# A second layer in three units of 192, 192 and 128 columns, and first keys scaled in halves

## The chip, the cores and the metric

The kernel runs on one core of a Trainium2 chip. The metric is the device time of one execution in microseconds; the kernel before takes 358.3 us (median of three runs, 358.1 to 358.67). TensorE (PE in the rows) multiplies matrices into PSUM, VectorE (DVE) and ScalarE (ACT) work on SBUF and PSUM, GpSimd (POOL) on SBUF, and SyncE (SP) issues the DMAs, which sixteen DMA engines carry out.

## What is computed

Attention on 8 batches of 8 heads (576 tokens, 64 columns a head, a mask by blocks of 64 tokens), and a soft mixture of experts on its output:

```python
scores = scale * q @ k.T                        # masked by blocks of 64
x = softmax(scores) @ v                         # as 4608 rows of 512
logits = x @ phi                                # 4608 x 32: 8 experts x 4 slots
slot_input = softmax(logits, over the rows).T @ x
h = relu(slot_input[e] @ w1[e])                 # 4 x 1024 for each expert
slot_out[e] = h @ w2[e]                         # 4 x 512
out = softmax(logits, over the slots) @ slot_out
```

All numbers are float32. `out` has 4608 rows of 512 columns; in the kernel it is written turned, 1152 rows of 2048 numbers, and the host turns it back.

## The kernel before

The attention goes over 32 pairs of heads, m = 0 to 31, as one list of steps in a fixed order: `at(t, fn, ...)` puts each step at a time (lines 843 to 937), the list is sorted, and each engine works it off in that order. Queries, keys and values come by `load_q`, `load_k` and `load_v`; `scale_k` multiplies the keys by 0.125 on GpSimd; `qk` and `qkb` form the scores. For the first pair this is the start of the kernel: SyncE issues keys, queries, the next keys, the next queries and the values, one after the other. Until the first keys are scaled, TensorE runs `WARM` = 8 matmuls on zeros (`warm`), and VectorE builds `stack` and `own` (lines 247 to 256), small constants that the second half uses.

The weights lie in `w`, 32 pieces of 128 x 2048 numbers (1 MB): 16 of the first layer, 16 of the second. 18 are loaded during the attention, 7 more into buffers that the last pairs leave (`places`), and the last 7 by `use(i)`, which reuses the buffer of a piece of the first layer as soon as that has been multiplied. The first layer (`up`, line 1064) takes 4 x 4 rounds.

The second layer (`down`, line 1082) goes by units: `NU` = 4 units of `CW` = 128 of the 512 columns. A unit is 16 steps; a step is four matmuls side by side, each of 128 rows by 32 columns of the array, over 128 columns of weights. When a unit is done, VectorE copies its sums to SBUF (`so_sb`), `finish(u)` adds the four strips up on TensorE (`summed`), and ScalarE copies the result (`s4[u]`). Then `emit(u, i)` forms parts of the output: `c` (the softmax over the slots, turned, in `cT`) for 2048 tokens (i = 0 and 1, the two token halves) against the 128 columns of the unit, four matmuls of 32 rows by 128 columns of the array side by side, 512 tokens each, into four banks of PSUM. ScalarE and VectorE copy two banks each to a staging buffer (one of the first layer's buffers that is free), and SyncE sends it: unit 0 as one DMA of 1 MB a part, later units as two of 512 KB, each after the second of its two copies. The last 512 tokens of all units go as parts '12' and '32', two units each. The order of the whole ending is written out in `ENDING` (line 63): a number is so many steps of `down` for the units behind unit 0, 'f1' is `finish(1)`, '10' is `emit(1, 0)`. The parts take turns in four banks ("x"); the last unit uses other banks as well. An engine works in its written order, so a copy that waits holds what is behind it on that engine.

Of the kernel before, what the change touches and what calls it, by code (L numbers as in the profile page):

```python
# [17 lines left out]
DM = H * D  # L18
# [22 lines left out]
WARM = 8  # L41
# [11 lines left out]
NPIECE = 32  # L53
# [177 lines left out]
def tile_attention_softmoe(  # L231
# [6 lines left out]
    w: bass.AP,  # L238
# [13 lines left out]
    for qd in range(2):  # L252
        for g in range(4):
            r = slice(NS * g, NS * (g + 1))
            s0 = 16 * qd + 4 * g
            nc.vector.tensor_reduce(out=own[r, qd:qd + 1], in_=stack[r, s0:s0 + 4], axis=AX.X, op=ALU.add)
# [51 lines left out]

    def load_piece(i, dst):
        place[i] = dst  # L310
        nc.sync.dma_start(out=dst, in_=w[i])
        pieces[i] = dst.rearrange("p (g f) -> p g f", g=4 if i < 16 else 16)
# [18 lines left out]
    with ExitStack() as c1:  # L331
# [91 lines left out]
        def scale_k(m):  # L423
            nc.gpsimd.tensor_scalar(  # L424
                out=area(f"ks{m % NQB}"), in0=area(f"ks{m % NQB}"), scalar1=SCALE, scalar2=0.0, op0=ALU.mult, op1=ALU.add
            )
# [515 lines left out]
    with ExitStack() as c2:  # L942
# [42 lines left out]
        def use(i):  # L985
# [3 lines left out]
            if fetched[0] < NPIECE:  # L989
# [19 lines left out]
        def emit(u, i):  # L1009
            ot = stage[no[0] % len(stage)]  # L1010
            no[0] += 1
            pss = []
            if (u, i) in ((NU - 1, 0), (NU - 1, 2)):
                pss += [nextbank("h") for g in range(2)]
                pss += [nextbank("so") for g in range(2, 4)]
            if (u, i) != (NU - 1, 2):
                pss += [nextbank("x") for g in range(4)]
            todo = [(s4[u], cT[:, i, 0:16, :])] if i < 2 else [(x, cT[:, :, 16:18, :]) for x in (s4[u - 1], s4[u])]
            m = 512 if i < 2 else 128
            n = m * len(todo)  # L1020
            lo = 256 * u + 128 * i
            if (u, i) == (NU - 1, 0):
                for h in range(2):
                    for g in range(4):
                        r = slice(NS * g, NS * (g + 1))
                        nc.tensor.matmul(
                            pss[4 * h + g][:, 0:256], lhsT=s4[u][r, :], rhs=cT[r, i, 8 * h:8 * h + 8, :],
                            start=True, stop=True, tile_position=(NS * g, 0),
                        )
                    for g in range(4):  # L1030
                        o = 1024 * h + 256 * g
                        (nc.vector.tensor_copy if g % 2 else nc.scalar.copy)(
                            out=ot[:, o:o + 256], in_=pss[4 * h + g][:, 0:256]
                        )
                        if g % 2:
                            nc.sync.dma_start(out=out[lo:lo + 128, o - 256:o + 256], in_=ot[:, o - 256:o + 256])
                return
            for x, (a, c) in enumerate(todo):
                for g in range(4):
                    r = slice(NS * g, NS * (g + 1))  # L1040
                    nc.tensor.matmul(  # L1041
# [123 lines left out]
```

## Time and profile before

| | |
|---|---|
| median of three runs | 358.3 us |
| the profiled execution: span | 357.1 us |
| around the span, in the median | 1.2 us |
| first scores start | 4.51 us |
| second layer starts | 320.48 us |
| first output sent | 328.01 us |
| last matmul of the output ends | 349.4 us |
| DMA queue falls idle | about 354.5 us |

The span runs from the first to the last instruction of the core. The rows that the prediction rests on stand in a section of their own below. In a row of the timeline the first number is the start, the second how long the group lasts, then engine, line, operation, tiles and shapes, the count, and in brackets how long the engine had been idle and what ended that. Each matmul on float32 stands as two records.

### The profile page before, as it was taken

Reading aid. Unit: us, or ns where it says so; the run is one execution under the profiler, and the core shown is the slowest. Engines: PE = TensorE matmul, PEld = TensorE weight load, DVE = VectorE, ACT = ScalarE, POOL = GpSimd, SP = SyncE. Lnnn points to the kernel's source line nnn. Section 1 sums busy time; section 2 is a strip of 40 time slices with the busy share of each in tenths; the row PEclk is TensorE's granted clock in tenths of the full one; section 3 lists DMA queues with packets and bytes.
Section 4 is the critical chain, followed back from the end, with each engine's and each line's share of the span. In section 5 each row is a group of like instructions: output and inputs, shape, how many; then the busy total and the mean of one; then the engine's idle time right before and its main releaser. Section 6 shows DMA issues by size and latency. Waiting matters only on the chain.

```text
span 357.1 us, 14425 instructions
## 1 busy us (share of the span) xinstructions
PE 342.2 (96%) x5724; PEld 237.1 (66%) x5724; DVE 261.5 (73%) x748; ACT 272.0 (76%) x869; POOL 205.0 (57%) x471
## 2 busy tenths in 40 slices
PE   8999999999999999999999999999999999999991
PEld 3767776677666766776767676776677677436750
DVE  4977777868887888777877887788888777462552
ACT  3988989888988898889888988899888875121441
POOL 3886767666766676567656766676687582000000
PEclk9999999999999999999999999999999999999996
DMA  6566526563664365743843556428333189999897
GB/s 198 182 211 229 163 74 212 199 225 101 184 224 133 102 218 186 249 106 114 292 135 101 204 195 211 148 70 312 127 104 102 36 253 331 375 397 397 327 373 298
DMA packets 29938, 72.29 MB, mean 202 GB/s; under 512 B 6960, under 2 KB 15280, under 8 KB 25520
## 3 DMA queue, kind: packets, MB, share of 16 engines
q1 hardware_dynamic: 29872, 71.38, 57.8%
q8 instruction: 45, 0.74, 0.8%
q14 instruction: 21, 0.17, 0.1%
HBM read 61.93 MB, written 9.44 MB: 200 GB/s over the span
## 4 chain that ended last, share of the span: by engine, by line
PE 79%; DVE 10%; POOL 5%; issue 3%; ACT 1%; DVEq 0%; POOLq 0%
PE one L592 15%; PE one L554 14%; PE one L464 7%; PE duo L464 7%; PE one L602 6%; PE one L485 5%; DVE stat L507 5%; POOL arena L534 4%; PE one L1088 4%; PE one L326 4%; PE duo L485 3%; PE one L1041 2%; PE one L623 2%; PE one L792 2%; DVE arena L392 1%
## 5 line engine op out<-in xcount | busy, mean ns | idle before, releaser
L534 POOL TENSOR_SCALAR arena<-arena,stat 128x512 f32<-128x512 f32 (+6 forms) x288 | 152.2, 544 | 30.8 <-DVE one L505 13.2
L517 ACT ACTIVATE arena<-one,stat 128x512 f32<-128x512 f32 (+5 forms) x194 | 93.9, 501 | 8.4 <-DVE stat L507 7.0
L390 ACT COPY arena<-one 128x384 f32<-128x384 f32 (+2 forms) x170 | 79.2, 503 | 26.8 <-PE one L554 21.3
L554 PEld LDWEIGHTS one<-ident,arena 64*128 64x128 f32 x1600 | 65.6, 138 | 33.4 <-ACT arena L390 9.0
L554 PE MATMUL one<-ident,arena 64*128 64x64 f32 x1600 | 76.3, 228 | 3.5 <-DVE arena L392 2.1
L507 DVE TENSOR_REDUCE stat<-one 128x1 f32<-128x512 f32 (+5 forms) x194 | 78.3, 436 | 1.7 <-PE one L485 0.6
L592 PE MATMUL one<-arena 128*64 128x256 f32 (+2 forms) x640 | 76.1, 384 | 0.0
L392 DVE COPY arena<-one 128x384 f32<-128x384 f32 (+3 forms) x106 | 56.4, 541 | 23.6 <-PE one L592 17.6
L517 ACT ACTIVATE arena<-duo,stat 128x384 f32<-128x384 f32 (+1 forms) x94 | 59.6, 640 | 7.0 <-DVE stat L523 5.6
L507 DVE TENSOR_REDUCE stat<-duo 128x1 f32<-128x576 f32 (+1 forms) x63 | 53.9, 855 | 13.3 <-PE duo L485 7.9
L592 PEld LDWEIGHTS one<-arena 128*64 128x64 f32 x640 | 41.1, 137 | 29.8 <-issue 18.2
L527 POOL TENSOR_SCALAR stat<-stat 128x2 f32<-128x2 f32 (+1 forms) x96 | 18.7, 195 | 55.0 <-ACT arena L517 50.9
L485 PE MATMUL one<-arena 64*64 64x256 f32 (+3 forms) x512 | 42.0, 303 | 0.0
L517 ACT ACTIVATION_READ_ACCUMULATOR arena<-one,stat 128x1 f32 x194 | 41.3, 213 | 0.0
L485 PE MATMUL duo<-arena 64*64 64x288 f32 x256 | 38.3, 417 | 0.0
L464 PE MATMUL one<-arena 64*128 64x512 f32 (+1 forms) x132 | 38.1, 636 | 0.0
L485 PEld LDWEIGHTS one<-arena 64*64 64x64 f32 x512 | 35.7, 133 | 2.2 <-ACT arena L517 0.4
L464 PE MATMUL duo<-arena 64*128 64x384 f32 x124 | 28.0, 529 | 0.4 <-ACT arena L517 0.4
L602 PE MATMUL one<-arena 128*64 128x64 f32 x620 | 24.9, 227 | 0.4 <-ACT arena L390 0.4
L602 PEld LDWEIGHTS one<-arena 128*64 128x64 f32 x620 | 20.6, 137 | 5.9 <-ACT xn L390 2.7
L424 POOL TENSOR_SCALAR arena<-arena 128x576 f32<-128x576 f32 x32 | 21.5, 672 | 3.6 <-DMA arena<-in_k 3.0
L523 DVE RECIPROCAL stat<-stat 128x2 f32<-128x2 f32 (+1 forms) x96 | 15.8, 165 | 7.2 <-POOL stat L527 6.9
(157 smaller groups left out, 382.8 us busy)
## 6 DMA issues: line engine op xcount, KB each, us to landing
arena<-in_w SPq DMA_DIRECT2D x31, 1024.0 KB, 7.2
arena<-in_k SPq DMA_DIRECT2D x32, 288.0 KB, 3.1
arena<-in_q SPq DMA_DIRECT2D x32, 288.0 KB, 3.2
arena<-in_v SPq DMA_DIRECT2D x32, 256.0 KB, 3.5
out<-arena SPq DMA_DIRECT2D x12, 512.0 KB, 4.5
out<-arena SPq DMA_DIRECT2D x2, 1024.0 KB, 5.6
arena<-in_v SPq DMA_DIRECT2D x32, 32.0 KB, 3.4
xarea<-in_w SPq DMA_DIRECT2D x1, 1024.0 KB, 8.0
```

The lines of the kernel that those rows point to most:

```text
L390: nc.scalar.copy(out=out, in_=in_)
L392: nc.vector.tensor_copy(out=out, in_=in_)
L424: nc.gpsimd.tensor_scalar(out=area(f"ks{m % NQB}"), in0=area(f"ks{m % NQB}"), scalar1=SCALE, scalar2=0.0, op0=ALU.mult, op1=ALU.add)
L464: nc.tensor.matmul(scores(t + str(j), m)[o, a:e], lhsT=q[r, lo + o.start:lo + o.stop], rhs=k[r, a:e], start=True, stop=True)
L485: nc.tensor.matmul(o, lhsT=a, rhs=b, start=True, stop=True)
L507: nc.vector.tensor_reduce(out=st[:, 0, u:u + n], in_=sc, axis=AX.XY if x == "8" else AX.X, op=ALU.max, negate=True)
L517: nc.scalar.activation(out=pr, in_=sc, func=AF.Exp, bias=st[:, 0, u:u + 1], accum_out=st[:, 1, u:u + 1],)
L527: nc.gpsimd.tensor_scalar(out=st[:, 2, c], in0=st[:, 1, c], scalar1=EPS, scalar2=1.0, op0=ALU.add, op1=ALU.mult)
L534: nc.gpsimd.tensor_scalar(out=pr, in0=pr, scalar1=st[:, 2, u:u + 1], scalar2=0.0, op0=ALU.mult, op1=ALU.add)
L554: nc.tensor.transpose(out=trbank(m, g)[i][:, 64 * n:64 * n + 64], in_=prob(m, x)[r, 128 * c:128 * c + 128], identity=ident[r, r],)
L592: nc.tensor.matmul(xps[m, 0][64 * j:64 * j + 64, lo:hi], lhsT=vs(m)[:, j, c, :], rhs=rhs, start=a, stop=z, skip_group_check=True,)
L602: nc.tensor.matmul(xps[m, 1][64 * j:64 * j + 64, 0:64], lhsT=vs(m)[:, j, c, :], rhs=arena[:, lo:lo + 64], start=(c == 0), stop=(c == NQ - 1),)
```

## The change

The second layer is cut into `UNITS` of 192, 192 and 128 columns. Steps of the units of 192 columns multiply 192 columns each. The weights of the second layer become 18 pieces in place of 16 (seven for a unit of 192: ten steps' slices of 192 columns to a piece, the last piece shorter), so nine are loaded by `use` in place of seven, and six staging buffers are left in place of eight. `finish` is called three times; for a unit of 192 ScalarE makes two copies, of 128 columns and of 64.

The parts are now: for each of the units of 192 two parts as before (128 columns, a token half each: '00', '01', '10', '11') and one of its last 64 columns with both token halves side by side ('0s', '1s'), eight matmuls of 32 rows by 64 columns of the array (`short`); 'A', the last 512 tokens of both units of 192 (384 numbers a bank); '20' in quarters and '21' in halves for the unit of 128; and 'B', its last 512 tokens. All parts of 512 numbers a bank are sent in halves of 512 KB, unit 0's too. `form` holds the matmuls and `send` the copies and DMAs; an entry with 'm' only forms, one with 'c' only sends, so A is formed ahead of `finish(2)` and copied behind it.

At the start, `scale_k(0)` scales one half of the keys' columns on VectorE and the other on ScalarE; the eight reductions that make `own` come after it on VectorE; the first queries come in two DMAs, their first 128 columns and the rest; `WARM` is 7.

```diff
-WARM = 8
+WARM = 7
-NU = 4
-CW = 128
+UNITS = ((0, 192), (192, 192), (384, 128))
-ENDING = (3, 'f0', 2, '00', 6, '01', 8, 'f1', 3, '10', 6, '11', 6, '12', 'f2', 3, '20', 6, '21', 5, 'f3', '30', '32', '31')
+ENDING = (2, 'f0', 2, '00', 3, '01', 3, '0s', 9, 'f1', 3, '10', 4, '11', 3, '1s', 3, 'mA', 'f2', 'cA', '20', 'B', '21')
...
         def load_q(m):
             b, p = divmod(m, NP)
-            nc.sync.dma_start(out=area(f"q{m % NQB}"), in_=qT[b, p])
+            cuts = (0, 128, S) if m == 0 else (0, S)
+            for lo, hi in zip(cuts, cuts[1:]):
+                nc.sync.dma_start(out=area(f"q{m % NQB}")[:, lo:hi], in_=qT[b, p][:, lo:hi])
...
         def scale_k(m):
+            if m == 0:
+                x, h = area("ks0"), S // 2
+                nc.vector.tensor_scalar(out=x[:, 0:h], in0=x[:, 0:h], scalar1=SCALE, scalar2=None, op0=ALU.mult)
+                nc.scalar.mul(out=x[:, h:S], in_=x[:, h:S], mul=SCALE)
+                own_slots()
+                return
...
         def finish(u):
+            n = UNITS[u][1]
             ps = nextbank("h")
             summed(ps, so_sb[u])
-            s4[u] = t2.tile([128, CW], F32, name=f"s4_{u}")
-            nc.scalar.copy(out=s4[u], in_=ps[:, 0:CW])
+            s4[u] = t2.tile([128, 128], F32, name=f"s4_{u}")
+            nc.scalar.copy(out=s4[u], in_=ps[:, 0:128])
+            if n > 128:
+                nc.scalar.copy(out=s4s[:, 64 * u:64 * u + 64], in_=ps[:, 128:192])
...
+        def short(pss, u, x, c):
+            for g in range(4):
+                r = slice(NS * g, NS * (g + 1))
+                for h in range(2):
+                    rhs = c(r, h)
+                    n = rhs.shape[1] * rhs.shape[2]
+                    nc.tensor.matmul(
+                        pss[g][64 * h:64 * h + 64, x:x + n], lhsT=s4s[r, 64 * u:64 * u + 64], rhs=rhs, start=True, stop=True,
+                        tile_position=(NS * g, 64 * h),
+                    )
...
+            for g in range(len(pss)):
+                (nc.vector.tensor_copy if g % 2 else nc.scalar.copy)(out=ot[:, n * g:n * g + n], in_=pss[g][:, 0:n])
+                if n in (256, 512) and g % 2:
+                    h = slice(n * (g - 1), n * (g + 1))
+                    nc.sync.dma_start(out=out[rows, h], in_=ot[:, h])
+            if n in (128, 384):
+                nc.sync.dma_start(out=out[rows, o:o + 4 * n], in_=ot[:, 0:4 * n])
...
         def down(u, n):
             hT = hTs[n // 8, n // 4 % 2]
+            lo, w = UNITS[u]
...
-                    so[u][NS * g:NS * (g + 1), 0:CW], lhsT=hT[:, 4 * (n % 4) + g, :], rhs=pieces[i][:, 4 * (n % 4) + g, :],
+                    so[u][NS * g:NS * (g + 1), 0:w], lhsT=hT[:, 4 * (n % 4) + g, :], rhs=slices[lo, 4 * n + g],
...
             elif isinstance(x, str):
-                emit(int(x[0]), int(x[1]))
+                if x[0] != "c":
+                    form(x.lstrip("mc"))
+                if x[0] != "m":
+                    send(x.lstrip("mc"))
```

## Rows read from the trace of the kernel before

**Rows 1.** The page, part 1: busy us (share of the span) and instructions.

```profile
PE 342.2 (96%) x5724; PEld 237.1 (66%) x5724; DVE 261.5 (73%) x748; ACT 272.0 (76%) x869; POOL 205.0 (57%) x471
```

**Rows 2.** Stretches of the ending: busy us by engine, granted clock, DMA share, GB/s.

```profile
327.50:329.00 1.50, 1.02 (x38) 1.02 (x37) 0.45 (x1) 0.19 (x1) 0.00 (x0) 1.00 0.67 284
331.50:332.50 1.00, 1.00 (x48) 0.97 (x42) 0.43 (x2) 0.00 (x0) 0.00 (x0) 1.00 0.10 41
335.00:335.60 0.60, 0.60 (x28) 0.40 (x19) 0.52 (x1) 0.26 (x1) 0.00 (x0) 1.00 0.12 41
...
342.50:347.50 5.00, 4.19 (x77) 2.47 (x78) 2.25 (x6) 2.15 (x7) 0.00 (x0) 1.00 1.00 401
347.50:348.00 0.50, 0.50 (x17) 0.50 (x17) 0.50 (x3) 0.39 (x2) 0.00 (x0) 1.00 0.56 221
348.00:354.50 6.50, 1.38 (x14) 0.52 (x9) 2.22 (x5) 1.72 (x4) 0.00 (x0) 0.78 1.02 405
```

**Rows 3.** Timeline of the DMAs that SyncE issues in the ending.

```profile
328.01 4.08 SPq L1057 DMA_DIRECT2D out<-arena  x2
334.98 3.45 SPq L1054 DMA_DIRECT2D out<-arena  x4
```

**Rows 4.** Timeline of TensorE in the ending.

```profile
320.48 4.33 PE L1088 MATMUL one<-arena 128*32 128x128 f32 x152
...
326.53 0.62 PE L1088 MATMUL one<-arena 128*32 128x128 f32 x10
327.98 1.29 PE L1088 MATMUL one<-arena 128*32 128x128 f32 x38 [0.82 <-issue]
...
333.03 0.70 PE L1041 MATMUL one<-cT,s 32*128 32x512 f32 x2
...
334.10 1.52 PE L1088 MATMUL one<-arena 128*32 128x128 f32 x48
335.55 0.70 PE L1041 MATMUL one<-cT,s 32*128 32x512 f32 x2
...
345.15 0.42 PE L960 MATMUL one<-so_sb,stack 128*32 128x128 f32 x8 [0.42 <-DVE so_sb L1094]
```

**Rows 5.** Timeline of VectorE, then of ScalarE, in the ending.

```profile
324.22 0.29 DVE L1094 COPY so_sb<-one 128x128 f32<-128x128 f32 x1 [2.00 <-PE one L1088]
...
334.84 0.68 DVE L1051 COPY arena<-x 128x512 f32<-128x512 f32 x1
...
334.19 0.58 ACT L1049 COPY arena<-one 128x512 f32<-128x512 f32 x1 [1.41 <-PE x L1041]
...
345.64 0.27 ACT L1003 COPY s<-one 128x128 f32<-128x128 f32 x1 [1.05 <-PE one L960]
```

**Rows 6.** Timeline of the start; landings of first queries and phi; ScalarE's 576 columns.

```profile
3.70 0.67 POOL L424 TENSOR_SCALAR arena<-arena 128x576 f32<-128x576 f32 x1 [1.82 <-DMA arena<-in_k]
5.96 0.67 POOL L424 TENSOR_SCALAR arena<-arena 128x576 f32<-128x576 f32 x1 [0.71 <-DMA arena<-in_k]
3.15 1.28 DVE L256 TENSOR_REDUCE own<-stack 32x1 f32<-32x4 f32 x8
0.99 3.59 PE L431 MATMUL one<-idle 128*128 128x512 bf16 x8 [0.99 <-DVE mrun L279]
4.51 2.08 PE L464 MATMUL one<-arena 64*128 64x512 f32 x4
7.94 1.13 PE L464 MATMUL one<-arena 64*128 64x512 f32 x4
...
1.17 0.42 SPq L403 DMA_DIRECT2D arena<-in_q  x1
...
DMA to landing us min/median/max: 3.1/3.1/3.1
...
DMA to landing us min/median/max: 2.7/2.7/2.7
...
L295 ACT ACTIVATE c_all<-c_all 128x576 f32<-128x576 f32 x2 | 1.4, 705 | 2.2 <-DVE c_all L290 2.2
```

**Rows 7.** Groups by line, the block of scores at 230 us: count, busy us, mean ns.

```profile
L485 PE MATMUL one<-arena 64*64 64x256 f32 (+3 forms) x16 | 1.3, 303 | 0.0
```

More of the change, by code (lines that the diff above doesn't have):

```diff
@@ L52 @@
     LATE0 += n
-NPIECE = 32
 PIECE = 2048
@@ L251, in tile_attention_softmoe, with own_slots @@
     own = const.tile([128, 2], F32, name="own")
[L252 to L256, printed above, removed]
+    def own_slots():
+        for qd in range(2):
+            for g in range(4):
+                r = slice(NS * g, NS * (g + 1))
+                s0 = 16 * qd + 4 * g
+                nc.vector.tensor_reduce(out=own[r, qd:qd + 1], in_=stack[r, s0:s0 + 4], axis=AX.X, op=ALU.add)
     idle = const.tile([128, 128], BF16, name="idle")
@@ new lines, in tile_attention_softmoe @@
+        s4s = t2.tile([128, 128], F32, name="s4s")
+        no = [0]
+        formed_at = {}
+        def short(pss, u, x, c):
+            for g in range(4):
+                r = slice(NS * g, NS * (g + 1))
+                for h in range(2):
[5 more added lines that the diff above has]
+                    )
@@ new lines, in full, with form @@
+        def full(pss, a, x, c):
+            for g in range(4):
+                r = slice(NS * g, NS * (g + 1))
+                rhs = c[r]
+                n = 512 if len(rhs.shape) == 3 and rhs.shape[1] == 16 else 256 if len(rhs.shape) == 3 else 128
+                nc.tensor.matmul(
+                    pss[g][:, x:x + n], lhsT=a[r, :], rhs=rhs, start=True, stop=True, tile_position=(NS * g, 0),
+                )
+        def form(name):
+            u = int(name[0]) if name[0] in "012" else 0
+            if name == "20":
+                pss = [nextbank(t) for t in ("h", "h", "so", "so", "x", "x", "x", "x")]
+            elif name == "B":
+                pss = [nextbank(t) for t in ("h", "h", "so", "so")]
+            else:
+                pss = [nextbank("x") for g in range(4)]
+            n = {"A": 384, "B": 128, "20": 256}.get(name, 512)
+            if name == "A":
+                for k, a in enumerate((s4[0], s4[1], s4s)):
+                    full(pss, a, 128 * k, cT[:, :, 16:18, :])
+            elif name == "B":
+                full(pss, s4[2], 0, cT[:, :, 16:18, :])
+            elif name == "20":
+                for k in range(2):
+                    full(pss[4 * k:4 * k + 4], s4[u], 0, cT[:, 0, 8 * k:8 * k + 8, :])
+            elif name[1] == "s":
+                short(pss, u, 0, lambda r, h: cT[r, h, 0:16, :])
+            else:
+                full(pss, s4[u], 0, cT[:, int(name[1]), 0:16, :])
+            formed_at[name] = pss, n
@@ L1010, in emit, with send @@
+        def send(name):
+            pss, n = formed_at.pop(name)
             ot = stage[no[0] % len(stage)]
             no[0] += 1
[L1012 to L1041, printed above, removed]
-                        pss[g][:, m * x:m * (x + 1)], lhsT=a[r, :], rhs=c[r], start=True, stop=True,
-                        tile_position=(NS * g, 0),
-                    )
-            halves = i < 2 and u > 0
-            for g in range(4):
-                dst = ot[:, n * g:n * g + n]
-                if g % 2 == 0:
-                    nc.scalar.copy(out=dst, in_=pss[g][:, 0:n])
-                else:
-                    nc.vector.tensor_copy(out=dst, in_=pss[g][:, 0:n])
-                if halves and g % 2:
-                    h = slice(1024 * (g // 2), 1024 * (g // 2) + 1024)
-                    nc.sync.dma_start(out=out[lo:lo + 128, h], in_=ot[:, h])
@@ L1055, in emit @@
[L1055 to L1060 removed]
+            if name in "AB":
+                rows, o = slice(1024, 1152), 1536 * (name == "B")
+            else:
+                lo = 384 * int(name[0]) + 128 * "01s".index(name[1])
+                rows, o = slice(lo, lo + 128), 0
@@ L1113, in tile_attention_softmoe @@
             down(0, n)
-        steps = [(u, n) for u in range(1, NU) for n in range(16)]
+        steps = [(u, n) for u in range(1, len(UNITS)) for n in range(16)]
         for x in ENDING:
```

60 lines of the change are left out of this document (41 added, 19 removed).

## Prediction

> **What bounds the kernel now.** I read the busy times of the engines first: the reader is to see that TensorE is busy for nearly the whole span [rows 1], so that up to the last quarter of the second layer work saved elsewhere counts only where TensorE was waiting for it. Then the stretches of the ending, for the DMA share: once the last weights are in, the output (1152 rows of 2048 floats, 9.44 MB) is all that moves, and the queue runs full but for a thin stretch at 327.5 and holes at 331.5, 335.0 and 347.5 us [rows 2]. Then SyncE's list: a send is issued at 334.98, and the queue moves again from 335.6, some 0.7 us later [rows 2, 3]; it ran dry because no part of the output was ready. Last TensorE, VectorE and ScalarE in the ending, to see what a part waits for [rows 4, 5]. So the end is set by two things that hand over to each other: TensorE decides when parts are ready, the DMA engines how fast they leave. The start is a chain of its own: the first keys land, GpSimd scales them, the first scores start [rows 6].
>
> **Rates.** 152 records of the second layer take 4.33 us, some 0.27 of it the last one's own length; that is 0.0267 each, and a step (four matmuls, two records each) of 128 columns is 0.213 us. I take the time to go with the columns, as the four matmuls of a step run side by side: a step of 192 columns is 0.32. A part of 512 columns holds TensorE for 1.07 us (333.03 to 334.10) and starts 0.17 after the steps before it end (six steps, 1.28, then 335.55) [rows 4]. Its copies begin 1.16 after it does, its first half is sent 1.95 and its second 2.55 after, and VectorE leaves the last of its four banks 2.49 after (334.84 + 0.68 - 333.03) [rows 3 to 5]. Half a part is 0.524 MB; four of them fill the 5.0 us from 342.5, so 1.25 us each [rows 2].
>
> **Part 1, the start.** Removed: GpSimd's 0.67 us on 576 columns from 3.70, the keys' landing, to 4.37; the scores start at 4.51 [rows 6]. Added: 288 columns each on VectorE and ScalarE side by side. ScalarE takes 705 ns for 576 columns [rows 6]; half of that, 0.35, would be without a fixed share, so I take 0.41, and as much for VectorE, of which no row has this form. Ready at 4.11 in place of 4.37: 0.26 gained. The eight reductions of `own_slots` (1.28 us of VectorE [rows 6]) move behind the scaling, where VectorE has nothing to do until the first scores are there, at 6.6; they cost nothing, and without that cover they would delay the first row maximum by 1.28. The queries would now bind: they land 3.1 us after their issue at 1.17, at 4.29 [rows 6]. The split sends their first 128 columns ahead, as much as the 64 KB of phi, which land in 2.7 us [rows 6], so at 3.9: hidden. The second piece costs SyncE one more issue (0.42): the next keys, queries and values start 0.4 later. The next scores run at 7.94, and the second keys are scaled at 6.63 [rows 6], so this is hidden too. One warm-up matmul less (3.59 us for eight) ends them at about 4.0, ahead of the keys. Bounds: nothing (the queries bind) to 0.4; I take **-0.25 us**. TensorE works in order and nearly full from there on, so I let it pass to the end.
>
> **Part 2, the ending, TensorE.** The columns are the same: 64 steps of 0.213 (13.65 us) become 32 of 0.32 and 16 of 0.213 (13.65), and the parts keep their columns too. What moves is the order. I lay it out from the first step at 320.48 [rows 4]. Unit 0 ends at 325.60. VectorE's copy follows 0.33 later (324.22 after 16 steps before [rows 5]) and takes 0.36, between the 0.29 of 128 columns and half as much again [rows 5]; the slot sum runs at 326.4, two more steps follow, and part 00 starts at **327.54**. It leaves as halves at 329.5 and 330.1 (before: whole, at 328.01 [rows 3]). Part 01 could start 1.07 + 0.96 + 0.17 = 2.20 later, but its fourth bank is free only after 2.49 and some 0.06, and TensorE is held 0.35. With the same bookkeeping 01 is issued at 331.7 and 332.3, 0s at 334.2 and 334.8. Then nine steps (six of 0.32, three of 0.213: 2.56), the slot sum and three more steps stand ahead of part 10, which starts at 337.2 and leaves at **339.2**. Parts 11 and 1s follow at the copies' pace (held 0.45 and 0.30), A is formed at 344.2 (held 0.38), and the last slot sum comes at 345.05. That is where it was before, 345.15 [rows 4]: the hole of 1.1 us (10 records start at 326.53, the next at 327.98, released by nothing that the profile shows [rows 4]) and some 0.4 of waiting for the last unit's copy go, and 1.8 us of waits for banks and copies come.
>
> The Trainium skill says under TensorEngine Tiling, PSUM Bottleneck, that tiling speeds up the matmuls but not the copies out of PSUM, which may then bind. The trace agrees as far as it goes, with 2.49 us to empty a part against 2.20 to reach the next. By a reading without that rule TensorE would reach its last slot sum up to 1.5 us sooner.
>
> **Part 3, the ending, DMA.** The queue moves 0.7 us after an issue and 1.25 per half. Weights move until about 328.9 [rows 2]; what the smaller pieces of a unit of 192 shift of them stays ahead of 330.2, when 00 begins. 00, 01 and 0s then leave without a break until 337.7; 10 can begin at 339.9: **a hole of 2.2 us**. From there 10, 11 and 1s take until 347.4. ScalarE copies the last sums (0.27, and 0.49 after the sum, as 345.64 stands to 345.15 [rows 4, 5]) ahead of its two copies of A (0.48 each, from 0.58 for 512 columns [rows 5]), so A is issued at 346.7 and moves at 347.4, just in time. A, 20, B and 21 are 6 halves: 7.5 us, and the queue falls idle at **354.9**. Before, the last unit began to move at 348.0 with 5 halves left: 354.2, and the stretch to 354.5 is full [rows 2]. So **+0.7 us**. The error of each time in this chain is some tenths; I allow 0.9 either way.
>
> **Sum.** 0.70 - 0.25 = +0.45 us. The profiled span is 357.1, so I expect one of 357.55; what lies around it (358.3 - 357.1 = 1.2) stays: **358.7**. About 0.2% (0.72 us) is what a measurement of this kernel can tell from no change.
>
> **Rivals.**
> Part 10 comes sooner. If banks don't hold 01 (a last copy ends earlier than I take it, or the steps behind a part don't wait for its fourth matmul) and the steps cover VectorE's copies of both units' sums, 0.35 and two times 0.16 of waits go ahead of 10. The hole shrinks to 1.5 and the end comes to 354.2, with the start 358.05. If the queue also takes 1.21 per half the 12 halves behind the hole give back 0.5 more: **357.6**, faster. The holds behind 10 give nothing, as the queue is full there. For it: before, a part followed the last in 2.52 us with no wait [rows 4]. Against it: 2.52 is just the 2.49 of the copies, so it never came to the test, and the long stretches of the queue show 401 and 405 GB/s [rows 2].
> A hole like the one after 326.53 stays [rows 4]. TensorE waits for nothing that semaphores show, most likely for its own code, late behind a full queue. Its place would be between 0s and 10, where TensorE alone decides; its price is 1.1; it decides from the point where 10 leaves after 339.2, since then each tenth is a tenth of the end. **359.8**, slower. For it: the queue is as full. Against it: the same instructions now take 2 us more, so the code has longer to come.
> The two halves of a 64-column part run one after the other. Then 0s and 1s cost 2.1 each in place of 1.07, both on the path: **360.8**. The nearest row is the score matmuls on 64 rows by 64 columns: 16 records of 303 ns are done in 1.3 us [rows 7], near four at a time, so I take the halves as side by side.
> The Trainium skill says under TensorEngine Tiling, Available Configurations and Key Properties, that the array splits into eight tiles of 32 rows by 64 columns, and that tiles run independently. By that the halves cost nothing; no row here has such a tile.
> The start gives nothing: the queries bind, or the pace of the first scores (four records in 2.08 us where the next four take 1.13 [rows 6]) lasts longer after one warm-up matmul less. That takes the 0.25 and up to 0.5 more: **359.0 to 359.5**.
>
> **How the numbers follow.** Forecast 0.48 (same 0.35, slower 0.09, faster 0.04); part 10 sooner 0.24 (same 0.12, faster 0.12); the hole 0.11 (slower 0.09, same 0.02); serial halves 0.08 (slower); no start 0.09 (same 0.04, slower 0.05). Faster 0.16, same 0.53, slower 0.31. The forecast's own range is 357.8 to 359.6; the first rival and the hole widen it to 357.2 and 360.0, which leaves out the serial halves and the far ends.
>
> **What would show it.** The first scores at 4.25, not 4.51. Part 00's first send at 329.5 less the start's gain. TensorE held 0.3 to 0.45 ahead of 01, 11, 1s and A. A hole of about 2 us in the queue between 0s and 10, and next to none behind it. The last slot sum within 0.3 of 345.15. Wrong would be: no hole there, part 10 sent before 338, or a long idle stretch of TensorE that no semaphore ends.

## The result, and the profile after

| kernel | median us | runs from, to | ratio to before, 95% interval |
|---|---|---|---|
| before | 358.2 | 357.73, 359.22 | |
| changed | 360.83 | 359.89, 361.28 | 1.0068 [1.0051, 1.0085] |

Slower by 2.6 us; 358.7 was forecast, 357.2 to 360.0 was the range. The profiled execution of the changed kernel took 361.28 us with a span of 359.5. In the profiled executions whose time is on record the time is 1.8 to 1.9 us above the span. For the kernel before that time is not on record; with 1.8 us it would be 358.9, so the 1.2 that the prediction put around the span was probably the 1.8 less 0.6, by which its profiled execution was slower than its median. Single executions of one kernel differ by a microsecond and more, so differences of a few tenths below are read inside one trace (from one of its events to another), and whole times as medians.

The page of the changed kernel, part 1 [rows 1 of before]. TensorE is as busy as it was:

```profile
PE 343.3 (95%) x5603; PEld 236.3 (66%) x5603; DVE 261.9 (73%) x748; ACT 272.9 (76%) x871; POOL 205.5 (57%) x470
```

Timeline of the sends that SyncE issues in the changed kernel [rows 3]; the first two are 0.6 us apart, the halves of part 00:

```profile
330.18 14.91 SPq L1093 DMA_DIRECT2D out<-arena  x12
347.05 0.33 SPq L1095 DMA_DIRECT2D out<-arena  x1
```

TensorE's timeline in the changed kernel [rows 4]: first step, first unit's slot sum, parts 00, 01, 0s and 10, last slot sum:

```profile
321.15 6.03 PE L1123 MATMUL one<-arena 128*32 128x192 f32 x144
327.11 0.53 PE L982 MATMUL one<-so_sb,stack 128*32 128x192 f32 x8
...
328.22 0.70 PE L1053 MATMUL one<-cT,s 32*128 32x512 f32 x2
...
330.41 0.70 PE L1053 MATMUL one<-cT,s 32*128 32x512 f32 x2
...
332.93 0.66 PE L1043 MATMUL one<-cT,s4s 32*64 32x512 f32 x4
...
337.73 0.70 PE L1053 MATMUL one<-cT,s 32*128 32x512 f32 x2
...
345.50 0.42 PE L982 MATMUL one<-so_sb,stack 128*32 128x128 f32 x8
```

Stretches of the changed kernel's ending [rows 2]: busy us by engine (PE, PEld, DVE, ACT, POOL), granted clock, DMA share, GB/s:

```profile
337.50:339.00 1.50, 1.50 (x28) 0.54 (x24) 0.07 (x1) 0.20 (x2) 0.00 (x0) 1.00 0.96 380
339.00:340.50 1.50, 1.50 (x38) 1.30 (x32) 1.22 (x2) 0.96 (x2) 0.00 (x0) 1.00 0.13 46
340.50:342.00 1.50, 1.50 (x32) 0.66 (x25) 0.99 (x2) 1.03 (x2) 0.00 (x0) 1.00 1.03 421
...
355.00:356.00 1.00, 0.00 (x0) 0.00 (x0) 0.00 (x0) 0.00 (x0) 0.00 (x0) 0.50 0.82 334
356.00:357.00 1.00, 0.00 (x0) 0.00 (x0) 0.00 (x0) 0.00 (x0) 0.00 (x0) 0.50 0.07 29
357.00:358.00 1.00, 0.00 (x0) 0.00 (x0) 0.00 (x0) 0.00 (x0) 0.00 (x0) 0.50 0.07 29
358.00:359.00 1.00, 0.00 (x0) 0.00 (x0) 0.00 (x0) 0.00 (x0) 0.00 (x0) 0.50 0.01 4
```

The same stretches at the end of the kernel before:

```profile
354.00:355.00 1.00, 0.00 (x0) 0.00 (x0) 0.00 (x0) 0.00 (x0) 0.00 (x0) 0.50 0.53 213
355.00:356.00 1.00, 0.00 (x0) 0.00 (x0) 0.00 (x0) 0.00 (x0) 0.00 (x0) 0.50 0.06 25
356.00:357.00 1.00, 0.00 (x0) 0.00 (x0) 0.00 (x0) 0.00 (x0) 0.00 (x0) 0.50 0.00 0
```

The forecast hole is there, at 339.0 to 340.5. But the lines to look at are the last ones. One engine that works alone makes a mean DMA share of 1/16, 0.06. Each send is split into 16 shares, and the trace notes when each has landed. After the change the last send's first share lands at 356.06 us, the fifteenth at 356.78 and the last at 358.65: for 1.9 us **one of the 16 engines works alone**. Before, it is 354.80 for the first and 356.00 for the last, but there two shares are late, by 0.97 and 1.21 us, and the other fourteen lie within 0.38. (Two engines for half of the microsecond from 355.0 make the same 0.06.) The "full" queue of the prediction was the common pace of the other engines. The trace does not name the engine of a share; that it is the same one, send after send, is read from one share in sixteen being late by nearly the same time.

So the two profiled executions differ as follows: the first step of the second layer starts 0.67 later (321.15 against 320.48), from there to the first share of the last send it takes 34.90 against 34.32 us, and from the first to the last share 2.60 against 1.21. Together the last share lands 0.67 + 0.58 + 1.39 = 2.64 later. The span grows by 2.4, as what follows the last share takes 0.85 in place of 1.07. The profiled execution of the changed kernel is the slowest of its six, so it shows more than the typical difference.

### The profile page after: what moved, and what is told of

It reads as the page before. It is cut to its first block, busy times and chain, and to the rows that moved or that the text cites. A ratio compares the mean times of both kernels' runs of the same rounds, so it can differ in the third digit from the quotient of the medians.

```text
span 359.5 us, 14198 instructions
## 1 busy us (share of the span) xinstructions
PE 343.3 (95%) x5603; PEld 236.3 (66%) x5603; DVE 261.9 (73%) x748; ACT 272.9 (76%) x871; POOL 205.5 (57%) x470
## 4 chain that ended last, share of the span: by engine, by line
PE 80%; DVE 9%; POOL 4%; issue 3%; ACT 2%; DVEq 0%; POOLq 0%; ACTq 0%
PE one L614 17%; PE one L576 14%; PE one L486 7%; PE duo L486 6%; PE one L624 6%; PE one L507 5%; PE one L1123 4%; PE one L340 4%; DVE stat L529 4%; PE duo L507 3%; POOL arena L556 3%; PE one L645 2%; PE one L1053 2%; PE one L814 1%; DVE arena L406 1%
```

## Experiments

Twelve kernels change a part or undo it, then four more hold TensorE back by a known time. The kernel before ran beside each of them on the same chip, and the ratios are to those runs. "Order" is the time from the first step of the second layer to the first share of the last send, "late" from that share to the last one, both from the kernel's trace, in us.

| kernel | median us | ratio, 95% interval | order | late |
|---|---|---|---|---|
| before | 358.2 | | 34.32 | 1.21 |
| e1_start | 358.62 | 1.0003 [0.9989, 1.0017] | 34.16 | 1.28 |
| e3_two | 358.06 | 0.9985 [0.9968, 1.0002] | 34.03 | 1.30 |
| f1_before60 | 358.59 | 1.0014 [1.0002, 1.0026] | 35.17 | 0.89 |
| f4_pool | 358.23 | 1.0006 [0.9989, 1.0023] | 34.01 | 1.45 |
| g4_halves | 358.49 | 1.0004 [0.9983, 1.0025] | 33.65 | 1.54 |
| h_before_6 | 358.21 | 0.9993 [0.9975, 1.0012] | 34.73 | 0.74 |
| h_before_11 | 359.52 | 1.0024 [1.0005, 1.0044] | 35.71 | 0.57 |
| changed | 360.83 | 1.0068 [1.0051, 1.0085] | 34.90 | 2.60 |
| e2_ending | 359.96 | 1.0048 [1.0022, 1.0073] | 34.96 | 2.47 |
| e4_shift | 360.2 | 1.0046 [1.0028, 1.0063] | 34.98 | 1.71 |
| f2_after60 | 360.07 | 1.0053 [1.0038, 1.0069] | 34.99 | 2.08 |
| f3_after100 | 360.1 | 1.0055 [1.0042, 1.0067] | 35.48 | 1.48 |
| g1_after120 | 360.25 | 1.0055 [1.0034, 1.0075] | 35.08 | 2.05 |
| g2_order | 360.7 | 1.0070 [1.0046, 1.0093] | 36.29 | 1.72 |
| g3_repair | 359.64 | 1.0039 [1.0020, 1.0059] | 35.34 | 1.42 |
| h_after_6 | 360.05 | 1.0047 [1.0027, 1.0067] | 36.12 | 1.27 |
| h_after_11 | 360.79 | 1.0056 [1.0034, 1.0077] | 37.20 | 0.80 |

**Which part of the change costs.** `e1_start` is the kernel before with the change's start alone:

```
-WARM = 8
+WARM = 7
+            cuts = (0, 128, S) if m == 0 else (0, S)          # queries in two pieces
+            if m == 0:                                        # keys in halves, own_slots behind
+                nc.vector.tensor_scalar(out=x[:, 0:h], ...)
+                nc.scalar.mul(out=x[:, h:S], ...)
+                own_slots()
```

> The kernel before with the start of the changed kernel alone (first keys in halves, own behind them, first queries in two DMAs, seven warm-up matmuls). If the start keeps its gain: first scores near 4.16 us, the second layer's first step 0.35 earlier than 320.48, median 0.25 to 0.35 below the kernel before. If the start itself sets the attention back, as the changed kernel's first step at 321.15 suggests: that step at 321 or later and a median 0.3 to 0.7 above the kernel before.

`e2_ending` is the changed kernel with these lines undone.

> The changed kernel with the start of the kernel before. If the start keeps its gain, this is 0.3 slower than the changed kernel: 2.9 us above the kernel before. If the start costs 0.7 by the second layer, this is faster than the changed kernel by about that: 1.9 above the kernel before. First step of the second layer at 320.5 if the attention is undisturbed; a hole of 1.3 to 2.2 us in the DMA queue ahead of part 10 in either case.

`e3_two` is the kernel before with the weights in two input tensors, as the change has them:

```
-    nc.sync.dma_start(out=dst, in_=w[i])
+    nc.sync.dma_start(out=dst, in_=w1[i] if i < 16 else w2[i - 16])
```

> The kernel before with its weights in two input tensors, as the changed kernel has them, and nothing else. The changed kernel's time is 1.78 us above its span, the kernel before 1.0 to 1.2. If the further tensor makes that: median 0.6 to 0.7 above the kernel before, the span as before. If not: within 0.2 of the kernel before.

The ending alone costs 0.5%; the start by itself and the tensors move nothing that can be measured. And with either start, the changed ending has an order term of 34.9 to 35.0 where the old one has 34.0 to 34.3.

**Where TensorE's code lies.** The page of the changed kernel lists 44 packets of kind "instruction" on queue q8, 0.72 MB, so 16 KB each, all through the run. They are read here as TensorE's code: they come sooner or later as TensorE gets more or fewer instructions, in the runs that follow. `e4_shift` moves all of TensorE's work to later places:

```
-                xps["w"], lhsT=idle[:, 0:128], rhs=idle[:, 0:64].unsqueeze(1).broadcast_to([128, 8, 64]), ...
+                xps["w"][0:32, 0:40], lhsT=idle[:, 0:32], rhs=idle[:, 0:40], ...
-WARM = 7
+WARM = 85
```

> The changed kernel with 85 warm-up matmuls of 40 columns in place of 7 of 512, the same 3 us of TensorE at the start but 156 more instructions ahead of all others. Theory of one late DMA engine: the last output lands 1.9 us after fifteen of its sixteen shares, since TensorE's code comes by the same engine and its last load (344.8 us) falls behind the last hole of the queue; 156 instructions earlier it falls into or near the hole at 339 to 340.5, the last landing is less than 1 us behind the others, and the span is some 1 to 1.4 us shorter than the changed kernel's. Rival (the engine is late whatever the code does): no change of the lag, within 0.4 us of the changed kernel.

Its median is some 0.6 us below that of the changed kernel, but the intervals of the two ratios overlap, and `e2_ending` is as low without any shift. The late share is 1.71 in place of 2.60, not under 1 as expected. In the changed kernel a fetch begins at 344.84 and takes 1.65 us; the shares of the send of 342.36 are the first behind the hole that are far apart, 345.96 for the first and 348.61 for the last, where those of the send before it lie within 0.42. In `e4_shift` the last fetch begins at 346.6, and it is the send of 343.87 whose last share falls back. The DMA view of 344 to 347 us in the changed kernel has that one fetch, the line with "instruction" (packets, MB, share of 16 engines' time: 3.4% of 16 engines for 3 us is a little over half of one engine's time):

```profile
q1 hardware_dynamic: 326, 1.15, 95.4%
q8 instruction: 1, 0.02, 3.4%
```

Three more runs put the code elsewhere: `f2_after60`, `f3_after100` and `g1_after120` are the same edit with 37 matmuls of 96 columns, 57 of 62 and 67 of 52.

> The changed kernel with 37 warm-up matmuls of 96 columns in place of 7 of 512: 60 TensorE instructions more, nothing else. Theory (one of the 16 DMA engines carries TensorE's code too and falls behind; a fetch that lands behind the last hole of the queue is never caught up): the fetch that landed at 344.8 is asked for by 338 and lands in the hole at 339 to 340.5, none follows, and the last send's 16 shares land within 0.8 us of each other in place of 2.6, so that the time is 1.2 to 1.9 us lower, 359.0 to 359.6. Rival (the late share belongs to the sends of the new ending, their sizes or number): the last share stays 1.7 to 2.6 us behind the first, and the time is 360.2 to 360.8.

> The changed kernel with 57 warm-up matmuls of 62 columns in place of 7 of 512: 100 TensorE instructions more, nothing else. Theory of the late DMA engine: the fetch that landed at 344.8 is asked for at 337 and lands in the hole; if one more is needed behind it, it lands near 350 and the last share is late again by 1 to 2 us. So either the shares land within 0.8 us of each other and the time is 359.0 to 359.6, or a fetch shows near 350 and the time is 360 to 361; a late share with no fetch behind 341 would speak against the theory. Rival (the sends themselves): 360.2 to 360.8 whatever the fetches do.

> The changed kernel with 67 warm-up matmuls of 52 columns in place of 7 of 512: 120 TensorE instructions more, nothing else. With 60 and 100 more, the fetches of TensorE's code landed at 342.5 and 340.2 us, and the last 16th share of the transfers behind them was late by some 2 us from there on. Theory (a fetch that lands in a full queue makes one DMA engine late, one that lands in a hole costs nothing): with 120 more the fetch lands at about 339.5, in the hole ahead of part 10; if none follows, the last send's shares land within 0.9 us of each other in place of 1.5 to 2.6, and the time is 358.7 to 359.4. Rival (the last share is late whatever the fetch does): 360.0 to 360.3.

The fetch of `f2_after60` did not land in the hole, where it was expected, but at 342.5: then the send of 339.55 has its shares within 0.26 us, that of 341.03 has its last one 2.47 behind. In `f3_after100` the last fetch begins at 340.2, with the hole just over, and the late share stays at 2.17, then 1.5; no other fetch follows. (A late share with no fetch behind 341 was to speak against the theory. By the letter it does; but this fetch took until 341.67, and the queue was full again from 340.0.) In `g1_after120` one lands in the hole, at 339.2, and the shares behind the hole are 0.6 to 1.0 apart; but a further one comes at 348.1, and from the send of 346.40 on the last share is 2.26 behind. In five places out of five one share falls back at the fetch, by 1.4 to 2.2 us where the send before it gives a measure (all but `f3_after100`). In the kernel before it is less: behind the fetches at 340.90 and 345.52 two shares fall back, by 0.2 to 0.9 us each. That a fetch in the full queue leaves an engine behind is what these traces show. That the time falls when it is gone they do not show, because no shift tried left the stretch behind the hole without a fetch: the times of 359.0 to 359.6 and 358.7 to 359.4 that the theory gave did not come, and 360.07 to 360.25 is as near to what its rivals gave.

**Whether the late engine sets the end.** The other way round: let the other fifteen engines run out of work for a time. `h_after_6`, `h_after_11`, `h_before_6` and `h_before_11` have the same edit in both kernels, with 6 or 11 idle matmuls into the bank of the last slot sum, which then overwrites it:

```
             ps = nextbank("h")
+            if u == 2:                     # NU - 1 in the kernel before
+                fill(ps, 6)
             summed(ps, so_sb[u])
```

> The changed kernel with six idle matmuls of 512 columns (some 1.3 us) ahead of the slot sum of the last unit; they write the bank that the sum overwrites. Theory (the late DMA engine sets the end): A, 20, B and 21 go out 1.3 us later, fifteen shares of the last send land 1.3 us later, the sixteenth where it was, as its engine catches up in the hole; the distance from the first to the last share falls from about 2 to about 1 us, and the time rises by 0 to 0.4 us over the changed kernel's 360.0 to 360.8. Rival (the common pace of the queue sets the end): the distance stays, and the time is 361.4 to 362.1.

> The changed kernel with eleven idle matmuls (some 2.35 us) at the same place. Theory (the late DMA engine sets the end): the late engine has caught up, the shares land within 0.6 us of each other, and the time rises by 0.4 to 1.2 us, to 360.6 to 361.8; of the 2.35 us at least one is absorbed. Rival (common pace): 362.4 to 363.2.

> The kernel before with six idle matmuls (some 1.3 us) ahead of the slot sum of the last unit, the same edit. There the last step comes 10.33 us ahead of the first share of the last send in every kernel, and the last share is 1.2 to 1.5 us behind the first. Theory (late engine): the first share moves by 1.3 us, the last by 0.3 to 1.0, so the time is 358.6 to 359.4. Rival (common pace): 359.4 to 359.9.

> The kernel before with eleven idle matmuls (some 2.35 us) at the same place. Theory (late engine): the shares land within 0.6 us of each other, and the time is 1.4 to 2.0 us above before, 359.5 to 360.2: then the changed ending, which costs 1.9 us, and a hold of 2.35 us in the old one come to the same. Rival (common pace): 360.5 to 361.0.

Stretches of `h_after_6`, in which part A goes out at 347.35 and a hole opens ahead of it:

```profile
347.50:349.00 1.50, 1.50 (x21) 1.38 (x19) 1.50 (x6) 1.38 (x6) 0.00 (x0) 1.00 0.63 266
...
355.00:356.00 1.00, 0.00 (x0) 0.00 (x0) 0.00 (x0) 0.00 (x0) 0.00 (x0) 0.50 0.85 348
356.00:357.00 1.00, 0.00 (x0) 0.00 (x0) 0.00 (x0) 0.00 (x0) 0.00 (x0) 0.50 0.06 25
357.00:358.00 1.00, 0.00 (x0) 0.00 (x0) 0.00 (x0) 0.00 (x0) 0.00 (x0) 0.50 0.00 0
```

and of `h_after_11`:

```profile
347.50:349.00 1.50, 1.12 (x17) 0.96 (x16) 0.28 (x1) 1.41 (x5) 0.00 (x0) 1.00 0.07 27
...
356.00:357.00 1.00, 0.00 (x0) 0.00 (x0) 0.00 (x0) 0.00 (x0) 0.00 (x0) 0.50 0.98 401
357.00:358.00 1.00, 0.00 (x0) 0.00 (x0) 0.00 (x0) 0.00 (x0) 0.00 (x0) 0.50 0.24 94
```

In `h_after_11` the stretch at 347.5 has a share of 0.07: the late engine alone, catching up while the others wait, and at the end nobody works alone for long. From the send ahead of this hole to the send behind it the late share goes from 2.50 to 0.22 us, in `h_after_6` from 2.48 to 1.22. The sends are the same, so it is not their sizes or their number that make a share late. Counted from the first step, the last share of the last send lands 37.50 us later in the changed kernel, 37.39 with the hold of 1.3 us and 38.00 with that of 2.35 (36.69 to 37.43 in the other kernels with the new ending in this order); the first share moves by 1.22 and 2.30. The medians say the same: 360.05 with 1.3 us of TensorE thrown away, no slower than the changed kernel; with 2.35 it is 0.7 above that (0.3 by the ratios). In the changed kernel the late engine sets the end.

In the kernel before the same edit says less. The last share lands 35.53 us after the first step, then 35.47 and 36.28, and 1.3 us thrown away can't be seen in the median (ratio 0.9993), less than the 0.3 us that was the least expected; of 2.35 us, 0.0024 of 358.5, or 0.9, arrives, less than the 1.4 to 2.0 expected. But the first share moves by only 0.41 and 1.39, not by the whole hold. TensorE waits there 0.42 us for VectorE's copy in any case [rows 4], so that the last slot sum comes only 0.91 and 1.99 later, counted from the last step; and in these two traces TensorE's stop behind part 00 (the stretch of 1.1 us below) is 0.27 and 0.26 us long in place of 0.82. Counted from the last step the first share lands 0.95 and 2.05 later, the last one 0.48 and 1.41. So in the kernel before late shares take up about half a microsecond of a hold, not all of it.

**The hole ahead of part 10.** `g2_order` forms part 10 one part sooner:

```
-ENDING = (2, 'f0', 2, '00', 3, '01', 3, '0s', 9, 'f1', 3, '10', 4, '11', 3, '1s', 3, 'mA', ...)
+ENDING = (2, 'f0', 2, '00', 3, '01', 12, 'f1', 3, '10', 3, '0s', 4, '11', 3, '1s', 'mA', ...)
```

> The changed kernel with part 0s behind part 10 instead of ahead of unit 1's last nine steps: part 10 is formed one part sooner, the work is the same. Theory (the queue ends late because TensorE has done too little of the work by the time at which the queue runs dry; the order of the parts only moves the hole): part 10 is sent near 337.6 in place of 339.69, the hole of some 2 us comes ahead of it all the same, at 337 to 339, the last send goes out within 0.4 us of 352.1, and the time is 359.8 to 360.8. Rival (the hole is there because part 10 stands behind 0s, and its length goes straight to the end): the hole shrinks to under 0.8, the last send goes out at 350.5 to 351.2, and the time is 358.5 to 359.3.

Part 10 goes out at 337.49 in place of 339.69 (1.2 us sooner, counted from the first step), and the hole comes ahead of it all the same, and is longer:

```profile
336.00:337.00 1.00, 1.00 (x24) 0.40 (x20) 0.26 (x1) 0.31 (x1) 0.00 (x0) 1.00 0.06 25
337.00:339.00 2.00, 2.00 (x36) 0.86 (x24) 1.42 (x3) 1.25 (x3) 0.00 (x0) 1.00 0.36 147
```

(TensorE is busy for all of it.) The first shares of 01's second half and of 10 are 4.55 us apart, 1.25 of them 10's own; in the changed kernel it is 3.15 between 0s and 10. The order term rises to 36.29; of that, 0.88 is the last slot sum, which comes later there, as the parts 1s and A follow each other with no steps between. So the hole is not 0s standing in the way.

**TensorE's stretch of 1.1 us at 326.9.** `f1_before60` is the kernel before with 38 warm-up matmuls of 96 columns, which moves its code by 60.

> The kernel before, with 38 warm-up matmuls of 96 columns in place of 8 of 512: the same 3 us of warm-up, but 60 TensorE instructions more, so that every later instruction sits 60 places further on in TensorE's code. Theory (TensorE's idle stretch after 326.53 us waits for its own code, whose packet starts at 325.70 behind a full queue): the fetch is now asked for some 2 us sooner, the stretch of 1.1 us is gone, the last slot sum comes near 344.1 in place of 345.15, and the time falls by 0.3 to 1.0 us to about 357.7. Rival (the stretch has another cause, in the order of the work): it stays where it is, and the time is 358.4 as before.

The stretch did not go, it grew, and it moved in the work: TensorE's timeline in this kernel has it one step after the slot sum of the first unit and ahead of part 00, where before has it behind 00 [rows 4].

```profile
323.28 0.42 PE L960 MATMUL one<-so_sb,stack 128*32 128x128 f32 x8
323.50 0.41 PE L1088 MATMUL one<-arena 128*32 128x128 f32 x4
325.69 0.63 PE L1088 MATMUL one<-arena 128*32 128x128 f32 x12 [1.78 <-issue]
326.25 0.70 PE L1041 MATMUL one<-cT,s 32*128 32x512 f32 x2
```

Counted from the start of TensorE's records it stands behind the same number of matmul records, 5270, in before, `e1_start`, `e3_two`, `f4_pool` and here, although here 30 of these are new. And TensorE goes on 2.20 to 2.40 us after a fetch has begun: fetch at 325.70, 325.35, 325.47, 324.56 and 323.36, next record at 327.98, 327.75, 327.81, 326.76 and 325.69. It waits for its code. The theory was right in the cause and wrong in the effect: a shift doesn't bring the fetch sooner than the steps need it.

**The start.** `f4_pool` has the change's start in the kernel before, but with the first half of the keys on GpSimd, and VectorE's reductions where they were:

```
+                nc.gpsimd.tensor_scalar(out=x[:, 0:h], in0=x[:, 0:h], scalar1=SCALE, scalar2=0.0, ...)
+                nc.scalar.mul(out=x[:, h:S], in_=x[:, h:S], mul=SCALE)
```

> The kernel before with another form of the change's start: queries in two pieces, one warm-up matmul less, the first keys scaled in halves by GpSimd and ScalarE; VectorE has no instruction more than before and keeps its reductions at their old place. Theory (what the changed start gains is lost again near 22 us because VectorE has one instruction more ahead of its first long wait, and its next instructions are not there yet): the first scores start at 4.1 to 4.2, the row maximum near 22 us starts within 0.15 us of its scores, the second layer starts 0.4 us sooner than before, and the time is 357.9 to 358.2. Rival (the loss near 22 us comes with any early start, since something there happens at a fixed time): the row maximum starts at 22.2 again, and the time is 358.4 to 358.7.

VectorE's first row maximum after its wait near 22 us, in the kernel before, then the changed kernel, `e1_start` and `f4_pool` (start, duration, and in brackets the idle time ahead and what ended it):

```profile
22.38 0.76 DVE L507 TENSOR_REDUCE stat<-duo 128x1 f32<-128x576 f32 x1 [2.39 <-PE duo L485]
```

```profile
22.50 0.76 DVE L529 TENSOR_REDUCE stat<-duo 128x1 f32<-128x576 f32 x1 [2.83 <-ACT xarea L404]
```

```profile
22.23 0.76 DVE L517 TENSOR_REDUCE stat<-duo 128x1 f32<-128x576 f32 x1 [2.83 <-ACT xarea L392]
```

```profile
21.90 0.76 DVE L514 TENSOR_REDUCE stat<-duo 128x1 f32<-128x576 f32 x1 [2.38 <-PE duo L492]
```

In before and `f4_pool` it starts some 0.1 us after TensorE has posted the scores. In the changed kernel the scores are posted at 21.98 and it starts at 22.50; the idle time is 0.45 longer. The copy that the profile names there is no cause: in before the maximum started at 22.38 and the same copy ended at 22.60. So the gain of the start, 0.35 to 0.6 us at 7 us, is down to nothing or little behind this point wherever VectorE does part of the scaling, and is kept where it doesn't. What exactly holds VectorE isn't settled. That its next instructions are late is argued only from its one instruction more, and the traces don't bear it out: the other packets of kind "instruction", 8 KB each on queue q14, could hold VectorE's code, but none lands between the first scores and this row maximum (the next one begins at 23.42 us in the changed kernel, at 23.32 in `e1_start`). What the gain is worth at the end isn't settled either: `f4_pool` is at 1.0006, its interval from 0.9989.

**Together.** `g3_repair` is the changed kernel with the start of `f4_pool` and the code shift of `g1_after120`; `g4_halves` is `f4_pool` with parts 00 and 01 sent in halves (`halves = i < 2` in place of `halves = i < 2 and u > 0`), a try at a version faster than both.

> The changed kernel with both found losses mended: the first half of the first keys scaled by GpSimd instead of VectorE, with VectorE's reductions at their old place, and 67 warm-up matmuls of 52 columns in place of 7 of 512. Theory (0.45 us near 22 us and 1.2 to 1.9 us of the last late share are what the change costs beyond the 0.7 us of its order): the row maximum near 22 us starts within 0.15 us of its scores, the last send's shares land within 0.9 us of each other, the time is 358.3 to 359.0, at most 0.2% above the kernel before. Rival (the losses are elsewhere): 360 us.

> The kernel before with the start that showed no loss (queries in two pieces, first keys scaled in halves by GpSimd and ScalarE, one warm-up matmul less) and with parts 00 and 01 sent in halves, as the other parts are: a try at a version that is faster than both. Theory (in the old ending TensorE's last step sets the end, 10.33 us ahead of the first share of the last send in every kernel with it, so what leaves sooner at 327 to 332 only lengthens the hole behind it): the first send goes out 0.6 us sooner, the 10.33 us stay, and the time is 357.9 to 358.4. Rival (the queue's thin stretch at 327.5 still counts at the end): 357.3 to 357.8.

In `g3_repair` the row maximum starts 0.1 us after its scores (21.21), but a further fetch comes at 348.7 and the last share is 1.42 late; its median is 0.6 below that of `g1_after120`, though the two intervals overlap, and it is still slower than the kernel before by 0.2 to 0.6%. In `g4_halves` the last share lands 10.34 + 1.54 us after the last step; in the six kernels with the old ending and no hold the first number is 10.32 to 10.34. Both miss the times expected, 358.3 to 359.0 and, by 0.1 us, 357.9 to 358.4. `g4_halves` is no faster than the kernel before (1.0004). None of the kernels is.

## Why the prediction was wrong

**What bounds the kernel, and Part 3: the step that failed.** The prediction took the time at which the queue falls idle, 354.2 before and 354.9 after, added the difference to the span, and so let what lies behind that time pass as a constant. Rows 2 show the share at 1.02 to 354.5, and the page's span ends at 357.1: 2.6 us, and until 356.00 late shares were still landing. That rest is not constant. The time from the first to the last share of the last send grew from 1.21 to 2.60 us in the profiled pair, and over the runs of the table from 0.89 to 1.54 with the old ending to 1.42 to 2.60 with the new one (without the holds: means 1.28 and 1.94, so 0.7 us). Part of the reason is in the order: before had a hole at 347.5 [rows 2], behind its last fetch at 345.5, in which the late engines caught up part of their arrears; the change fills that hole, as the prediction said it would ("next to none behind it"), and with it the chance to catch up. What the new order saves there is not paid out. Across the hole the late share falls by 0.3 to 0.6 us in the six kernels with the old ending and no hold (before: 1.78 to 1.30); at the same place of the new ending without a hold it falls by 0.2 at most (changed: 2.81 to 2.59). The rest of the growth in the profiled pair was there already: behind the last fetch the late share is 2.65 in the changed kernel, 1.79 before. Why the fetch costs more there stays open.

**The order term.** +0.7 was forecast, from 354.2 to 354.9; measured are 34.90 to 34.99 in the changed kernel, `e2_ending`, `e4_shift` and `f2_after60` against 34.03 to 34.32 in before, `e1_start` and `e3_two`: +0.6 to +1.0. The means of all kernels without a hold, 34.2 with the old ending and 35.1 with the new one (without `g2_order`), differ by 0.9. Right in size, though single traces of the old ending differ by up to 1.5.

**Part 2, the timetable.** Less the 0.67 by which the first step came later, part 00 starts at 327.55 (forecast 327.54), 01 leaves at 331.69 (331.7), 0s at 334.20 (334.2), 10 at 339.02 (339.2), A at 346.38 (346.7), and the last slot sum is at 344.83 (345.05). The hole of 1.1 us in TensorE is gone as forecast; the steps of 192 columns use up code more slowly. The hold ahead of 01 shows as longer matmuls (0.95 in place of 0.70), not as idle time. Parts of 64 columns run their two halves side by side: the steps behind 0s start 1.04 us after it (332.93 to 333.97), those behind part 00 1.07 after that (328.22 to 329.29).

**Part 1, the start.** The first scores run at 4.16 in place of 4.51, somewhat sooner than the 4.25 forecast. "So I let it pass to the end" failed: 0.45 us of it are lost at 22 us on VectorE, and from there on the changed kernel is 0.1 us behind. That VectorE's eight reductions were hidden was right; that its own instruction more would cost nothing was not looked at. One sum is off: seven warm-up matmuls end at 4.13 (0.99 and 7/8 of 3.59), level with the scaled keys, not at about 4.0. Of the 0.67 at the first step no more than this is accounted for: in the nine traces with the new ending and VectorE's start or the old one it comes between 320.05 and 321.15, in before, `e1_start` and `e3_two` between 320.39 and 320.59, in `f1_before60` at 319.10 and in `h_before_11`, which has the start of before, at 322.18. So the profiled execution was one of the late ones.

**The rivals.** Part 10 sooner: its condition was not met, as the steps behind 01 start 1.41 us after it (330.41 to 331.82), 0.34 of it held by the banks; and when `g2_order` forms part 10 sooner by another way, there is no gain. The hole like 326.53's: not there. Serial halves: not so. The start gives nothing (359.0 to 359.5): so it came, but by luck. The queries did not bind, and the first four records take 2.08 us as before; the loss is at 22 us. And it is still 1.3 to 1.8 us below the result, without the term that was larger. No rival had the late engine in it, and the forecast of "slower" with 0.31 was too low for a change that fills the last hole of a queue.

**The sum, as measured.** Order +0.6, late share +0.7 to +1.4, start 0 in place of -0.25: 1.3 to 2.0, and the medians of `e2_ending` to `g1_after120` are 1.6 to 2.0 above before by their ratios. The changed kernel itself is 2.4 above by its ratio (1.8 to 3.0 by the interval). Whether the rest is chance or has a cause of its own stays open, as the intervals overlap.

## What to carry to other kernels

Where a queue is full to the end, read the last share of the last transfer, not the point at which the mean share falls: a mean of 0.06 for a microsecond or two can be one engine of sixteen that decides the time, and here 1.2 us more for the others was not felt. Ask which holes in the queue let such an engine catch up before filling them. A change that adds instructions to one engine, even warm-up ones, moves the places of its code fetches, so compare two or three shifts of the code before a difference of half a per cent is put down to the order of the work. Here the new ending was slower by 0.46 to 0.55% in all four shifts, so the loss is not that of one unlucky place.

## What the hardware showed that was not expected

- A 16 KB fetch of TensorE's code takes 0.9 to 1.2 us in most cases of the ending, 1.4 to 1.9 in some. In the full output queue of the new ending it leaves one of the 16 DMA engines behind the others (its share is 2.65, 2.47 and 2.26 us late behind the last fetch of the changed kernel, `f2_after60` and `g1_after120`), in the kernel before two of them by less. Most of these arrears stay for as long as the queue is full: 2.60 of the 2.65 are left at the end.
- TensorE went on 2.20 to 2.40 us after the beginning of the fetch it waited for, in five kernels, and the wait, 0.28 to 1.78 us by the page, is at a place of the code, not of the work.
- Throwing away 1.3 us of TensorE ahead of its last slot sum costs nothing that can be measured in the new ending (ratio 1.0047, against 1.0046 to 1.0068 without). In the old one it doesn't either (0.9993), but there 0.42 us of it fall into a wait.
- VectorE started 0.5 us after the scores it needs were posted, in kernels in which it has one instruction more at the start (`f4_pool`, without it: 0.1 us). Why is open.
